# Carrying an angle from chunk to chunk: an accumulating DMA of one row in place of a second matmul

## The chip, the core and the metric

The kernel runs on one NeuronCore of a Trainium2 chip. The metric is the device time of one launch in microseconds (us), from the first to the last instruction with what lies around it. Five engines work side by side, each through its own instructions in order: TensorE (PE) multiplies matrices, VectorE (DVE) and ScalarE (ACT) work elementwise, GpSimd (POOL) does small elementwise work and issues some DMAs, SyncE (SP) issues the other DMAs. They wait for one another by semaphores only.

## The reference

Two blocks follow each other. The first is a gated linear recurrence with complex gates, for 4 batches, 8 heads, 768 time steps and head size 48:

```python
mag = np.sqrt(a_re * a_re + a_im * a_im)
scale = np.minimum(mag, 0.999) / (mag + 1e-06)
a = (a_re + 1j * a_im) * scale          # the reference keeps the two parts apart
for t in range(S):
    S_state = a[:, :, t, :, None] * S_state + einsum('bhd,bhe->bhde', k[:, :, t], v[:, :, t])
    y[:, :, t] = einsum('bhd,bhde->bhe', q[:, :, t], S_state.real)
```

The second is a mixer on `x`, the `y` of all heads side by side (batch, 768 tokens, 384 channels):

```python
h = x.transpose(0, 2, 1) @ U @ V         # over tokens, rank 32
u = x + h.transpose(0, 2, 1)
out = u + np.maximum(u @ w_ch1, 0.0) @ w_ch2    # 384 -> 1536 -> 384
```

All inputs and the output are float32.

## The kernel before, in words

The 768 tokens of a batch are cut into 6 chunks of 128, so there are 24 chunks over the 4 batches. Tokens lie on the 128 partitions and the 384 channels (8 heads of 48) on the free axis. Chunks go through the gate work in groups: chunk 0 alone, chunk 1 alone, and then pairs (2, 3), (4, 5) and so on to (22, 23).

**The gates** (`gate_steps`). A gate is a complex number; the recurrence needs the running product of gates, so the kernel adds logarithms of magnitudes and adds angles. Steps s0 to s2 make the log magnitude `l` and the ratio whose arctangent is the angle (ACT functions Square, Ln, Exp; DVE between them). `after_each` (L301) multiplies `l` with a triangle (`es`) and `of_blocks` (L309 to L320) with block sums (`tot`), after copying `l` twice into `ll`. Step s4 (L326 to L329) makes the angle of each token's gate, in turns: `y`. Step s5 (L331 to L340) adds these angles along time. For one chunk, TensorE multiplies `y` with the triangle `prefix`, which sums each token's angle with all earlier ones of the chunk (L336), into the PSUM tile `ph`. A chunk that isn't the first of its batch also needs the angle at the end of the chunk before. That is row 127 of `F[:, (i-1) % 2]`, and a second matmul into the same `ph` adds it to all 128 tokens, with the constant `tail` (zero but for -1 in its last row) as the stationary operand (L338). Then ACT adds the constant MAGIC, which rounds the turns to whole numbers (L339), and DVE takes the fraction (L340). The result `F` is the negative of the angle's fraction of a turn, hence the -1 in `tail`. Step s6 turns both chunks of the group at once into sines and cosines: `n` (L348), and two `cs` (L349, L350).

`F` has two slots, one for even and one for odd chunks; `y` and the other gate temporaries have one buffer each, so the next group's Square into `y` waits for the last `ph` matmul of this group.

**The chunks.** `prep_steps` multiplies q and k with `es` and `cs` (`qkc`, DVE), transposes them on TensorE (`tr`, L380) and copies them out on ACT. `chain_steps` builds the attention matrix of a chunk in levels: `inner` matmuls (L412) alternate with DVE multiplications of `QK` (the line of the helper `mul`, L256), then `place` copies, `corners` (L443), `corner` (L453), keys (`ks`, L479), outputs (`yT`, L465 and L469), the state update (`dk`, L485) and the transposed output (`yr`, L497), which ACT copies to the chunk's `x`.

**The mixer** (`mixer_steps`) works on pairs of chunks: rank (L540), mixed (L550), transposes `uT`, 12 `up` tiles (L563) with a ReLU on ACT (`h`), 2 `down` tiles (L571), an addition on DVE (L574) and the output DMA from POOL (L575).

**The order.** Python emits these steps interleaved (`weave`), from streams with a begin and an end within a chunk's turn; the tile framework then schedules the instructions and sets each engine's order and semaphores. The mixer of the first batch begins once that batch's 6 chunks are done. The last mixer pairs, of the last batch, run alone at the end. POOL's queue carries the constants at the start, the `ll` copies from chunk 8 on, and the 24 output DMAs. All loads are issued by SP.

Of the kernel before, what the change touches and what calls it, by code (L numbers as in the profile page):

```python
# [9 lines left out]
FP = mybir.dt.float32  # L10
I32 = mybir.dt.int32
U32 = mybir.dt.uint32
AF = mybir.ActivationFunctionType
OP = mybir.AluOpType
PSUM = bass.MemoryType.PSUM

CH = 128
# [3 lines left out]
GC = 2  # L21
# [14 lines left out]
def kernel(  # L36
# [24 lines left out]
    nc = tc.nc  # L61
# [3 lines left out]
    DM = H * D  # L65
# [9 lines left out]
    MAGIC = 12582912.0  # L75
# [10 lines left out]
    def pool(name, bufs, **kw):  # L86
        return ctx.enter_context(tc.tile_pool(name=name, bufs=bufs, **kw))

    singles = pool("singles", 1)
# [19 lines left out]
    def where(i):  # L109
        return divmod(i, NCH)  # L110
# [21 lines left out]
    prefix = singles.tile([128, CH], FP, name="prefix")  # L132
# [3 lines left out]
    ident = singles.tile([128, 128], FP, name="ident")  # L136
# [3 lines left out]
    def column(nm, value):  # L140
        t = singles.tile([128, 1], FP, name=nm)
        nc.vector.memset(t, value)
        return t

    leps, lmax, tiny = column("leps", math.log(1e-6)), column("lmax", LNMAX), column("tiny", 1e-30)
    magic, fourth = column("magic", MAGIC), column("fourth", 0.25)

    tail = singles.tile([128, CH], FP, name="tail")
    nc.gpsimd.tensor_scalar(out=tail, in0=ident[:, 127:128].to_broadcast([128, CH]), scalar1=-1.0, scalar2=None,
                            op0=OP.mult)  # L150

    after = singles.tile([128, CH], FP, name="after")
    quads = prefix.rearrange("p (b t) -> p b t", t=4)
# [1 line left out]
                            in0=quads[:, :, 3:4].to_broadcast([128, CH // 4, 4]), in1=quads, op=OP.subtract)  # L155
# [9 lines left out]
    F = singles.tile([128, GC, DM], FP, name="F")  # L165
# [75 lines left out]
    def act(o, i, f, **kw):  # L241
        return nc.scalar.activation(out=o, in_=i, func=f, **kw)  # L242
# [3 lines left out]
    def queue(ins):  # L246

        if queued:
            behind(ins, queued[-1])
        queued[:] = [ins]  # L250

    def tact(*a, **kw):
        queue(act(*a, **kw))

    def mul(o, a, b):
        nc.vector.tensor_tensor(out=o, in0=a, in1=b, op=OP.mult)  # L256

    def heads(a):
        return a.rearrange("p (x d) -> p x d", d=D)
# [4 lines left out]
    def gate_steps(g):  # L264
        st = {}
        lo, hi = GROUPS[g]
        W = (hi - lo) * DM

        def tmp(nm):
            st[nm] = pt.tile([128, GC * DM], FP, tag=nm, name=nm)[:, 0:W]  # L270
            return st[nm]

        def s0():
            x, y = tmp("x"), tmp("y")
            act(x, T["ar", g], AF.Square)
            act(y, T["ai", g], AF.Square)
            nc.vector.tensor_tensor(out=x, in0=x, in1=y, op=OP.add)
            nc.vector.tensor_scalar(out=x, in0=x, scalar1=M2LO, scalar2=M2HI, op0=OP.max, op1=OP.min)

        def s1():  # L280
            queue(nc.scalar.preload_act_table_set("natural_log_exp_and_others"))
            x, y, l, n = st["x"], st["y"], tmp("l"), tmp("n")
            act(n, T["ar", g], AF.Abs)
            tact(l, x, AF.Ln)
            tact(x, l, AF.Exp, scale=0.5)
            nc.vector.tensor_tensor(out=x, in0=x, in1=n, op=OP.add)
            tact(y, l, AF.Exp, scale=-0.5, bias=leps)
            tact(y, y, AF.Ln, bias=1.0)

            act(l, l, AF.Relu, scale=-0.5, bias=lmax)  # L290
            nc.vector.scalar_tensor_tensor(out=l, in0=l, scalar=LNMAX, in1=y, op0=OP.subtract, op1=OP.add)  # L291

        def s2():
            x = st["x"]
            tact(x, x, AF.Ln)
            tact(x, x, AF.Exp, scale=-1.0)
            mul(x, x, T["ai", g])

        def after_each(i):
            ps = psT.tile([128, DM], FP, tag="t", padded_shape=[128, 512], name="es")  # L300
            nc.tensor.matmul(out=ps, lhsT=after, rhs=st["l"][:, (i - lo) * DM:(i - lo + 1) * DM], start=True, stop=True)  # L301
            T["es", i] = pe.tile([128, 2, DM], FP, tag="es", name="es")
            tact(T["es", i][:, 0], ps, AF.Exp)
            tact(T["es", i][:, 1], ps, AF.Exp, scale=-1.0)

        def of_blocks(i):
            l = st["l"][:, (i - lo) * DM:(i - lo + 1) * DM]
            ll = pkc.tile([128, H, 2, D], FP, tag="ll", name="ll")
            (nc.scalar.copy if i < NCH + GC else nc.gpsimd.tensor_copy)(out=ll, in_=heads(l).unsqueeze(2).to_broadcast([128, H, 2, D]))  # L309
            if g == 0:  # L310
                queue(nc.scalar.preload_act_table_set("natural_log_exp_and_others"))
            ps = psT.tile([128, H, 64], FP, tag="t", name="tot")
            for h in range(H):
                nc.tensor.matmul(out=ps[0:D2, h, 0:NTOT], lhsT=ll[:, h].rearrange("p u d -> p (u d)"), rhs=total,  # L314
                                 start=True, stop=True)
            tt = pTT.tile([D2, H * NTOT], FP, tag="T", name="T")
            for n in SIZES:
                m = CH // n
                T["T", i, n] = tt[:, H * FIRST[n]:H * (FIRST[n] + m)].rearrange("p (h b) -> p h b", h=H)
                tact(T["T", i, n], ps[0:D2, :, FIRST[n]:FIRST[n] + m], AF.Exp, scale=-1.0)  # L320

        def s4():
            queue(nc.scalar.preload_act_table_set("trig_and_small"))
            x, y = st["x"], st["y"]

            act(y, T["ar", g], AF.Sign, bias=tiny)  # L326
            tact(x, x, AF.Arctan)
            nc.vector.scalar_tensor_tensor(out=y, in0=x, scalar=math.pi / 4, in1=y, op0=OP.subtract, op1=OP.mult)
            act(y, y, AF.Identity, scale=1.0 / math.pi, bias=fourth)  # L329

        def s5(i):  # L331

            f = F[:, i % GC]
            first = where(i)[1] == 0
            ps = psT.tile([128, DM], FP, tag="t", padded_shape=[128, 512], name="ph")
            nc.tensor.matmul(out=ps, lhsT=prefix, rhs=st["y"][:, (i - lo) * DM:(i - lo + 1) * DM], start=True, stop=first)  # L336
            if not first:
                nc.tensor.matmul(out=ps, lhsT=tail, rhs=F[:, (i - 1) % GC], start=False, stop=True)  # L338
            act(f, ps, AF.Identity, bias=magic)  # L339
            nc.vector.scalar_tensor_tensor(out=f, in0=f, scalar=MAGIC, in1=ps, op0=OP.subtract, op1=OP.subtract)  # L340

        def s6():
            cs = pg.tile([128, GC, H, 2, D], FP, tag="cs", name="cs")
            for i in range(lo, hi):
                T["cs", i] = cs[:, i - lo]
            cs = cs.rearrange("p c h u d -> p (c h) u d")[:, 0:W // D]
            f = F.rearrange("p c m -> p (c m)")[:, lo % GC * DM:lo % GC * DM + W]
            act(st["n"], f, AF.Abs)  # L348
            tact(cs[:, :, 1], heads(f), AF.Sin, scale=-2.0 * math.pi)  # L349
            tact(cs[:, :, 0], heads(st["n"]), AF.Sin, scale=-2.0 * math.pi, bias=quarter)  # L350

        each, blocks = ([lambda f=f, i=i: f(i) for i in range(lo, hi)] for f in (after_each, of_blocks))
        turns = [s4] + [lambda i=i: s5(i) for i in range(lo, hi)] + [s6]
        if g == 0:
            return [s0, s1, s2] + each, turns + blocks
        return [s0, s1, s2] + each + blocks, turns
# [251 lines left out]
    first = sum([mixer_steps(m, pu) for m in range((NT - NCH) // MC)], [])  # L608
# [83 lines left out]
```

## Time and profile before

| | |
|---|---|
| median of 3 runs (lowest to highest) | 881.14 us (879.32 to 882.34) |
| the profiled execution's own time | 880.63 us |
| its span, first to last instruction | 878.9 us |
| mean granted TensorE clock | 0.959 |
| ph matmul passes, L336 and L338 | 48 and 40 |
| DMA to HBM out of POOL's queue | 24, each 192 KB, 2.1 us to landing |

The profile is of one execution. "Busy" sums the time in which an engine executed; "x" gives a count. A float32 matmul shows as two instructions (passes), each with a weight load, which the profile lists as PEld and which overlaps other passes. Durations of matmuls include their way through the array, so back-to-back passes overlap in the records and the price of one more pass is read from a run of many. A line number with an arrow after a time, such as "[2.07 <-PE ph L338]", says how long the engine had been idle before the instruction and which instruction ended the wait.

### The profile page before, as it was taken

Reading aid. Unit: us, or ns where it says so; the run is one execution under the profiler, and the core shown is the slowest. Engines: PE = TensorE matmul, PEld = TensorE weight load, DVE = VectorE, ACT = ScalarE, POOL = GpSimd, SP = SyncE. Lnnn points to the kernel's source line nnn. Section 1 sums busy time; section 2 is a strip of 40 time slices with the busy share of each in tenths; the row PEclk is TensorE's granted clock in tenths of the full one; section 3 lists DMA queues with packets and bytes.
Section 4 is the critical chain, followed back from the end, with each engine's and each line's share of the span. In section 5 each row is a group of like instructions: output and inputs, shape, how many; then the busy total and the mean of one; then the engine's idle time right before and its main releaser. Section 6 shows DMA issues by size and latency. Waiting matters only on the chain.

```text
span 878.9 us, 24505 instructions
## 1 busy us (share of the span) xinstructions
PE 793.9 (90%) x11088; PEld 586.8 (67%) x11088; DVE 434.2 (49%) x621; ACT 465.2 (53%) x983; POOL 44.4 (5%) x67
## 2 busy tenths in 40 slices
PE   3657878888899999999999999999999999999997
PEld 2444656656677776866867867866867778575774
DVE  3577588789865635525536527427516343001010
ACT  7797787657654755745737628619615324020110
POOL 3000000010400000000000000000000000000000
PEclk9978879699899999999999999999999999999999
DMA  7442233242401400401301301301100000000000
GB/s 169 108 93 61 59 83 84 65 109 97 113 20 29 82 11 21 81 19 26 69 10 38 65 10 39 65 19 29 29 19 11 3 19 2 19 1 18 10 10 18
DMA packets 130904, 40.27 MB, mean 46 GB/s; under 512 B 126448, under 2 KB 127344, under 8 KB 130800
## 3 DMA queue, kind: packets, MB, share of 16 engines
q1 hardware_dynamic: 129264, 33.99, 17.4%
q0 software_dynamic: 1536, 4.72, 1.5%
q8 instruction: 87, 1.43, 0.7%
q14 instruction: 17, 0.14, 0.1%
HBM read 33.59 MB, written 4.72 MB: 44 GB/s over the span
## 4 chain that ended last, share of the span: by engine, by line
PE 75%; ACT 14%; DVE 6%; issue 3%; POOL 1%; DMA 0%; POOLq 0%; DVEq 0%; ACTq 0%
PE down L571 21%; PE up L563 19%; PE inner L412 6%; PE tot L314 4%; PE tr L380 4%; PE yT L465 4%; PE dk L485 3%; PE es L301 3%; PE yT L469 2%; PE ph L336 2%; PE ks L479 2%; ACT y L242 2%; DVE QK L256 1%; ACT n L242 1%; ACT cs L242 1%
## 5 line engine op out<-in xcount | busy, mean ns | idle before, releaser
L563 PE MATMUL up<-uT,w 128*128 128x256 f32 x864 | 210.6, 389 | 8.8 <-ACT h L242 5.5
L571 PE MATMUL down<-w,h 128*128 128x384 f32 x576 | 190.2, 487 | 0.0
L256 DVE TENSOR_TENSOR QK<-QK,T 96x1024 f32<-96x1024 f32 (+1 forms) x144 | 157.3, 1097 | 54.5 <-PE corners L443 38.1
L563 PEld LDWEIGHTS up<-uT,w 128*128 128x128 f32 x864 | 158.7, 192 | 33.5 <-ACT h L242 8.3
L571 PEld LDWEIGHTS down<-w,h 128*128 128x128 f32 x576 | 108.1, 190 | 71.3 <-issue 0.2
L574 DVE TENSOR_TENSOR x<-down,x 128x384 f32<-128x384 f32 x24 | 13.4, 557 | 215.3 <-PE down L571 215.3
L242 ACT ACTIVATE h<-up 128x256 f32<-128x256 f32 x144 | 55.0, 382 | 117.3 <-PE up L563 116.6
L382 ACT COPY QK<-tr 96x512 f32<-96x512 f32 x96 | 55.5, 582 | 73.5 <-PE tr L380 72.5
L412 PE MATMUL inner<-QK 96*32 96x32 f32 x6144 | 82.9, 203 | 10.8 <-DVE QK L256 5.3
L412 PEld LDWEIGHTS inner<-QK 96*32 96x32 f32 x6144 | 68.8, 114 | 34.9 <-issue 19.6
L380 PE MATMUL tr<-ident,qkc 128*96 128x128 f32 x384 | 66.0, 301 | 9.4 <-DVE qkc L256 8.1
L414 DVE COPY_PREDICATED DG<-mask,inner 128x256 f32<-128x256 int32 x96 | 42.3, 441 | 48.4 <-PE inner L412 46.9
L380 PEld LDWEIGHTS tr<-ident,qkc 128*96 128x96 f32 x384 | 45.1, 137 | 26.0 <-DVE qkc L256 9.5
L472 ACT COPY yTs<-yT 128x512 f32<-128x512 f32 x24 | 14.1, 587 | 81.2 <-PE yT L469 79.5
L465 PE MATMUL yT<-AT,VP 128*64 128x128 f32 x384 | 47.1, 303 | 3.0 <-ACT AT L457 1.5
L256 DVE TENSOR_TENSOR qkc<-qk,cs 128x768 f32<-128x768 f32 x48 | 44.5, 949 | 2.7 <-PE tr L380 1.9
L314 PEld LDWEIGHTS tot<-total,ll 128*96 128x96 f32 x384 | 39.0, 178 | 9.2 <-POOL ll L309 4.0
L314 PE MATMUL tot<-total,ll 128*96 128x63 f32 x384 | 40.7, 262 | 4.5 <-POOL ll L309 2.7
L437 ACT COPY AT<-DG 32x256 f32<-32x256 f32 x96 | 38.4, 400 | 9.1 <-DVE DG L414 8.2
L309 POOL COPY ll<-l 128x768 f32<-128x768 f32 x16 | 22.9, 1428 | 400.4 <-DVE l L291 256.8
L301 PE MATMUL es<-l,after 128*128 128x384 f32 x48 | 26.0, 633 | 12.8 <-DVE l L291 12.6
L465 PEld LDWEIGHTS yT<-AT,VP 128*64 128x64 f32 x384 | 28.8, 148 | 12.5 <-issue 9.3
(93 smaller groups left out, 949.4 us busy)
## 6 DMA issues: line engine op xcount, KB each, us to landing
ar<-in_a_re_dram SPq DMA_DIRECT2D x24, 192.0 KB, 3.5
ai<-in_a_im_dram SPq DMA_DIRECT2D x24, 192.0 KB, 3.2
qk<-in_q_dram SPq DMA_DIRECT2D x24, 192.0 KB, 2.9
qk<-in_k_dram SPq DMA_DIRECT2D x24, 192.0 KB, 3.4
VP<-in_v_dram SPq DMA_DIRECT2D x24, 192.0 KB, 2.6
raw<-in_moe_w_ch_dram SPq DMA_DIRECT2D x6, 768.0 KB, 4.6
raw<-in_moe_w_ch_dram SPq DMA_DIRECT2D x12, 384.0 KB, 3.7
out_dram<-x POOLq DMA_DIRECT2D x24, 192.0 KB, 2.1
```

Source lines behind the costliest of these rows:

```text
L242: return nc.scalar.activation(out=o, in_=i, func=f, **kw)
L256: nc.vector.tensor_tensor(out=o, in0=a, in1=b, op=OP.mult)
L301: nc.tensor.matmul(out=ps, lhsT=after, rhs=st["l"][:, (i - lo) * DM:(i - lo + 1) * DM], start=True, stop=True)
L314: nc.tensor.matmul(out=ps[0:D2, h, 0:NTOT], lhsT=ll[:, h].rearrange("p u d -> p (u d)"), rhs=total, start=True, stop=True)
L380: nc.tensor.transpose(out=ps[0:D2, j], in_=T["qkc", i][:, u, hh * HH + j].rearrange("p u d -> p (u d)"), identity=ident)
L382: nc.scalar.copy(out=T["QK", i][:, u, hh * HH:(hh + 1) * HH], in_=ps[0:D2])
L412: nc.tensor.matmul(out=ps[js, h], lhsT=k_of(h)[:, js], rhs=q_of(h)[:, js], start=True, stop=True, tile_position=(0, j * BLK))
L414: T["level"] = nc.vector.copy_predicated(out=DG[i % 2], mask=mask[:, n].unsqueeze(1).to_broadcast([128, H, BLK]), data=ps)
L437: nc.scalar.copy(out=AT[i % 2][js, :, js], in_=DG[i % 2][js])
L465: nc.tensor.matmul(out=y[u * DP:(u + 1) * DP, p], lhsT=vv[:, h], rhs=AT[i % 2][:, h], start=True, stop=(c == 0), tile_position=(0, u * DP))
L563: nc.tensor.matmul(out=ps, lhsT=w1[:, f, ff * 128:(ff + 1) * 128], rhs=st["uT"][:, f], start=(f == 0), stop=(f == KD - 1))
L571: nc.tensor.matmul(out=ps, lhsT=st["h"][:, ff, cc * CH:(cc + 1) * CH], rhs=w2[:, ff], start=(ff == 0), stop=(ff == KF - 1))
```

## The change

The tail matmul (L338) and its constant go. Instead, for every chunk that isn't the first of its batch, a DMA from POOL's queue adds row 127 of the last chunk's `F` to row 0 of this chunk's `y`, before the prefix matmul: what is in the first token's increment reaches all 128 tokens of the sum. The row is 384 numbers, 1.5 KB. For this `F` now holds the angle's fraction itself, not its negative: ACT takes `-ph` plus MAGIC, DVE adds `ph` where it took it away, and the sine's scale changes sign. There are 20 such chunks (24, less the first of each batch).

```diff
-    tail = singles.tile([128, CH], FP, name="tail")
-    nc.gpsimd.tensor_scalar(out=tail, in0=ident[:, 127:128].to_broadcast([128, CH]), scalar1=-1.0, scalar2=None,
-                            op0=OP.mult)
...
         def s5(i):
             f = F[:, i % GC]
-            first = where(i)[1] == 0
+            y = st["y"][:, (i - lo) * DM:(i - lo + 1) * DM]
+            if where(i)[1] > 0:
+                nc.gpsimd.dma_start(out=y[0:1], in_=F[CH - 1:CH, (i - 1) % GC], accum_op=OP.add)
             ps = psT.tile([128, DM], FP, tag="t", padded_shape=[128, 512], name="ph")
-            nc.tensor.matmul(out=ps, lhsT=prefix, rhs=st["y"][:, (i - lo) * DM:(i - lo + 1) * DM], start=True, stop=first)
-            if not first:
-                nc.tensor.matmul(out=ps, lhsT=tail, rhs=F[:, (i - 1) % GC], start=False, stop=True)
-            act(f, ps, AF.Identity, bias=magic)
-            nc.vector.scalar_tensor_tensor(out=f, in0=f, scalar=MAGIC, in1=ps, op0=OP.subtract, op1=OP.subtract)
+            nc.tensor.matmul(out=ps, lhsT=prefix, rhs=y, start=True, stop=True)
+            act(f, ps, AF.Identity, scale=-1.0, bias=magic)
+            nc.vector.scalar_tensor_tensor(out=f, in0=f, scalar=MAGIC, in1=ps, op0=OP.subtract, op1=OP.add)
...
-            tact(cs[:, :, 1], heads(f), AF.Sin, scale=-2.0 * math.pi)
+            tact(cs[:, :, 1], heads(f), AF.Sin, scale=2.0 * math.pi)
```

The scheduler orders the changed program anew, so other instructions change places too. In the changed program's order on POOL, the 20 row DMAs stand among the `ll` copies and the output DMAs; on TensorE the `ph` matmuls of a pair, which stood close together before in some groups, have other work between them, and those of chunks 2 and 4 stand later among the work of the chunks before.

## The prediction

> **What bounds the kernel now.** I read in this order: the busy shares, the busy times by stretch, what TensorE waits for, the phase tile, the time order around it.
>
> ```profile
> PE 793.9 (90%) x11088; PEld 586.8 (67%) x11088; DVE 434.2 (49%) x621; ACT 465.2 (53%) x983; POOL 44.4 (5%) x67
> ```
>
> The average hides two regimes. By stretch (us, then busy us and instructions of PE, weight loads, DVE, ACT, POOL, then granted clock):
>
> ```profile
> 0.00:216.00 216.00, 158.51 (x2886) 115.41 (x2886) 154.54 (x231) 160.98 (x320) 10.59 (x29) 0.86 0.39 92
> 216.00:770.00 554.00, 536.38 (x7820) 400.48 (x7821) 271.30 (x376) 290.44 (x628) 30.56 (x32) 0.99 0.15 35
> 770.00:879.00 109.00, 99.05 (x383) 70.86 (x383) 8.36 (x15) 13.83 (x36) 3.24 (x6) 1.00 0.03 11
> ```
>
> Until 216 us no engine is full (PE 73%, DVE 72%, ACT 75%): chains from engine to engine set the pace. From 216 to 770 us TensorE is 97% busy and no other engine passes 52%; what is taken from it there shortens the run. After 770 us the change issues nothing. The phase tile (duration min/median/max, first and last start):
>
> ```profile
> L338 PE MATMUL ph<-F,tail x40: 486/486/847, 39.8 to 657.3; 128*128 128x384 f32 x40
> L242 ACT ACTIVATE F<-ph,magic x24: 562/581/582, 16.9 to 657.8; 128x384 f32<-128x384 f32 x24
> L340 DVE SCALAR_TENSOR_TENSOR F<-F,ph x24: 542/553/559, 17.5 to 658.4; 128x384 f32<-128x384 f32 x24
> ```
>
> Forty rows are 20 tail matmuls in two passes each. 486 ns is latency; the price in a full queue is read from the chain, where passes of the same shape run back to back:
>
> ```profile
> 771.07 15.81 PE up L563 x72
> 786.87 15.48 PE down L571 x48
> ```
>
> So a 128x384 pass costs 15.48/48 = 0.3225 us, a matmul of two passes 0.645; an "up" matmul of two passes costs 15.81/36 = 0.44. The time order on ACT for the pair of chunks 2 and 3 shows how the tail stands in a serial chain:
>
> ```profile
> 65.54 0.94 ACT L242 ACTIVATE y<-y,fourth 128x768 f32<-128x768 f32 x1
> ...
> 69.78 0.58 ACT L242 ACTIVATE F<-ph,magic 128x384 f32<-128x384 f32 x1 [2.07 <-PE ph L338]
> ...
> 71.96 0.58 ACT L242 ACTIVATE F<-ph,magic 128x384 f32<-128x384 f32 x1 [0.27 <-PE ph L338]
> ...
> 73.95 0.85 ACT L242 ACTIVATE n<-F 128x768 f32<-128x768 f32 x1
> ```
>
> From the end of y (66.48) to n, the first reader of both finished chunks, 7.5 us pass. Read likewise: chunk 1 alone 4.2 us (38.28 to 42.51), chunks 4 and 5 10.2 (101.61 to 111.85), 6 and 7 11.1 (144.93 to 156.03), 8 and 9 6.0 (208.02 to 214.02).
>
> **What the Trainium skill says.** DMA: Bandwidth & Descriptors, "SWDGE vs HWDGE vs iDMA": accumulation in a DMA must be issued from GpSimd; so POOL's queue carries it. The same page, "Anatomy of one DMA — SWDGE (gpsimd) path": about 2.0 us fixed plus bytes over 436 GB/s, most of it the write's receipt. The trace agrees for the one POOL transfer it has, though that goes to HBM and doesn't accumulate:
>
> ```profile
> out_dram<-x POOLq DMA_DIRECT2D x24, 192.0 KB, 2.1
> ```
>
> TensorE: Matmul & The Clock Gate, "Step-by-step: what each phase is for": matmuls stay in program order and only weight loads are pulled ahead, so a matmul that waits for a DMA holds every later one. The trace agrees in kind: waits stand ahead of single matmuls with later work queued. SBUF — State Buffer, "Who interferes with whom": DVE and GpSimd exclude each other on a shared port pair for a whole instruction; POOL's ll copy shows it, 0.83 us at best and 6.64 us at worst. The out_dram issue, 0.54 us at the median and 0.77 at most, shows little of it.
>
> **The change part by part.**
>
> Removed: 20 tail matmuls. Chunks 1 to 5 and 7 (six) lie before 216 us. Fourteen belong to chunks 8 to 11, 13 to 17 and 19 to 23; 8 and 9 stand at 208 to 213 us, where the mixer's matmuls have begun to fill the queue. 14 x 0.645 = **9.0 us** of TensorE. Their weight loads run beside other passes, so they are worth nothing more. The tail tile's setup, one POOL instruction of 1.1 us at 5.1 us, gates no first matmul: POOL makes "after", which the first es needs, ahead of it. Worth nothing. The sign moves into ACT's scale and DVE's add: same instructions, 0.58 and 0.55 us, same shapes.
>
> Added: 20 DMAs of 1.5 KB (in the built program 16 runs of 24 numbers each). POOL pays 20 x 0.54 = 10.8 us in an engine 95% idle: nothing on the path. Issue to landing isn't in this trace for such a transfer: low end 2.0 us (the fixed part above; no reason for less), high end 3.5 (the slowest median row of the loads, ar, as the SDMA engines are 39% busy early). I take 2.1.
>
> Added waits. The first chunk of a group now runs y, DMA, ph; the second runs F of the first, DMA, ph. A pair is then 2.1 + ph 0.8 + F 0.58 + 0.55 + 2.1 + 0.8 + 0.58 + 0.55 + about 0.6 for hops = 8.7 us from y to n with warm passes, 9.0 with the first one cold. Against the measured spans:
> - Chunk 1: 0.1 + 2.1 + 1.65 (a cold ph) + 0.58 + 0.56 + 0.3 = 5.3 against 4.2: +1.1.
> - Chunks 2, 3: 9.0 against 7.5: +1.5.
> - Chunks 4, 5: 9.0 against 10.2: fits, 0. Chunks 6, 7 (one DMA): 7.4 against 11.1: fits, 0.
> - Chunks 8, 9: 8.7 against 6.0: 2.7 later, but TensorE has "up" work between.
>
> Behind a waiting ph stands the next row of TensorE; behind F on ACT stand the place copies and the next group's Square; behind the DMA on POOL stand ll copies (tot waits for these) and output stores (nobody does).
>
> Where the cover is: the built order keeps the ph matmuls apart now. Between ph(8) and ph(9) stand 15 inner at 0.02, 9 up at 0.44 and 8 corner at 0.086: 0.3 + 4.0 + 0.7 = 5.0 us of matmul time, against F 0.58 + 0.55 + DMA 2.1 + hops 0.3 = 3.5. For the later second chunks the same count gives 20 to 22 us, or 10.7 where a group straddles two batches' work; for first chunks 4.5 to 15 us after the last matmul that y can depend on. So after 216 us I cost the new waits at 0. Without that cover each would cost up to 3.5 us.
>
> Moved: before 120 us the built order puts ph(2) behind yT, dk, yr and a whole inner level of chunk 0/1, and ph(4) behind yr, where both stood ahead of them. I take +1.0 for this, bounds 0 and +14.7: dk began 6.3 us after ph(2) did (73.36 against 67.06), yr 8.4 after ph(4) (110.78 against 102.33). I take so little because work that is moved ahead (corners, place copies) needn't be done later.
>
> Given back: TensorE waited 22 of 652 us after 216; a shorter queue meets its producers sooner. I take 10% of the gain, 0.9 (0 to 2).
>
> Sum: -9.0 + 1.1 + 1.5 + 1.0 + 0.9 = **-4.5 us**. The profiled run took 880.63 us (span 878.9 and 1.7 around it), so it would take 876.1; the median of the runs, 881.14, is 0.5 above that run, so I forecast 876.6.
>
> **The rivals.**
> - *Everything early is hidden as well.* ACT idles 55 us before 216, so the 2.6 us may vanish: -9.0, or 872. With cold passes also saved (a tail of 1.35 us at 68.39) 869 is the low end.
> - *The DMA takes 3.5 us.* Chunk 1 +2.5, chunks 2 and 3 +4.3, chunks 4 and 5 +1.6: 8.4, with 1.9 given back and moved, against 9.0: +1.3, or 882.4. Chunks 8, 9 then need 4.9 of their 5.0 us. For it: loads land in 2.6 to 3.5 us. Against it: the row is tiny and stays in SBUF.
> - *Slower: the early order.* TensorE keeps its order, so ph(2) and ph(4), put behind yr, start when yr is done; cs, qkc and everything for the next chunks shift. At its full price 14.7 + 0.9 - 9.0 = +6.6, or 887.7. It decides from 60% of its price on, 9 us. For it: in the trace qkc starts at 76.38, 0.03 us after cs ends, so that group's chain had no slack. Against it: for chunks 4 and 5 cs ended at 114.25 and qkc started at 115.97.
> - *It doesn't do what it says:* excluded; in the built order no tail matmul is left and 20 row transfers stand on POOL.
>
> **How the numbers follow.** 0.3% (2.6 us) is about what a measurement of this kernel can tell from no change. Forecast with the first rival: 0.50, all faster. The slow DMA, or an early order at half its price: within 0.3%, 0.17. The early order at over three quarters, alone or with the slow DMA: 0.33, slower. I leave that much because the early stretch is a net of short chains whose order has changed throughout. Range 869 to 888: from the first rival's low end to the full price of the third. The likeliest case's own range is 872 to 878.5.
>
> **What would show it.** Right: no L338 rows; PE busy down by 11 to 20 us; y row transfers landing in 2.0 to 2.5 us; PE waits on them after 216 us under 2 us in all; 216 us's events 1 to 5 us later; the rest about 9 us shorter. Wrong: ph waits of over 1 us for a DMA late in the run, landing above 3 us, ACT idle ahead of F up by several us before 120 us, or the first mixer "up" over 8 us later than 205.8.

## The result and the profile after

Side by side on one chip, four runs each, the changed kernel took 882.38 us (881.51 to 884.08) and the kernel before 880.52 (879.32 to 882.34). The ratio is 1.0022, interval 0.9997 to 1.0046: no change that can be measured. It lies inside the predicted range (869 to 888), but the likeliest case, 4.5 us faster, did not come. A second pairing later (`after_again` below) gave 0.9999 [0.9973, 1.0026], with medians of 884.49 and 882.47 us. Every ratio here is taken over all runs but those more than 1.5% slower than their kernel's fastest, and so isn't the quotient of the two medians.

The profiled run of the changed kernel took 881.51 us, span 879.7, at a granted clock of 0.959 as before. Its busy line answers to the first one shown:

```profile
PE 786.9 (89%) x11048; PEld 586.2 (67%) x11048; DVE 437.8 (50%) x621; ACT 464.5 (53%) x983; POOL 55.7 (6%) x86
```

The 40 passes of the tail are gone, and TensorE is busy 7.0 us less (786.9 for 793.9). Yet the span is 0.9 us longer. The same three stretches of the changed kernel (columns as before: us, then PE, weight loads, DVE, ACT, POOL, granted clock):

```profile
0.00:216.00 216.00, 154.16 (x2828) 116.42 (x2828) 150.20 (x222) 156.19 (x314) 15.15 (x35) 0.87 0.38 91
216.00:770.00 554.00, 533.88 (x7840) 399.06 (x7840) 279.26 (x385) 294.44 (x633) 37.36 (x45) 0.99 0.15 35
770.00:879.00 109.00, 98.88 (x383) 70.70 (x381) 8.37 (x15) 13.83 (x36) 3.24 (x6) 0.99 0.03 11
```

Before 216 us fewer matmuls are done than before (2828 passes instead of 2886; at most 16 of these are tails): the kernel is behind. In the middle TensorE idles 20.1 us (554 less 533.88) where it idled 17.6. The new instructions, from the list of the phase tile `ph` (a "phase" below is a `ph` matmul) (duration in ns min/median/max, first and last start) and from the page's list of DMAs (KB each, median us from issue to landing):

```profile
L335 PE MATMUL ph<-y,prefix x48: 486/488/1010, 15.1 to 657.1; 128*128 128x384 f32 x48
L333 POOL DMA_DIRECT2D y<-F x20: 757/766/984, 38.5 to 638.5; - x20
```

```profile
y<-F POOLq DMA_DIRECT2D x20, 1.5 KB, 1.9
```

The tail rows are gone, the 20 row transfers are there, and one lands in 1.9 us at the median (1.8 to 4.0; three take 3.4 or more, those of chunks 1 and 8 and one at 571.86 us).

**Where the time went** is read from the chain of waits, which runs through the mixer's second "down" tile of every pair once TensorE is full. Its entries for the first, third and eighth pair (start us, us, what), before:

```profile
265.54 7.74 PE down L571 x24
...
393.41 7.74 PE down L571 x24
...
704.45 7.74 PE down L571 x24
```

and in the changed kernel:

```profile
268.54 7.74 PE down L568 x24
...
395.97 7.74 PE down L568 x24
...
704.28 7.74 PE down L568 x24
```

The changed kernel is 3.0 us behind at the first pair, 2.6 at the third, and 0.2 ahead at the eighth. So the full stretch gave back 3.2 us, where 11 tail matmuls of 0.645 us, 7.1 us, had gone, and the loss before it took as much. (The price holds: in the trace of the kernel before, each of these 11 tails holds the next pass of TensorE back by 0.645 us.) This division of the run is used for all kernels below, so here are all of them, from one trace each. The columns: start of `n` of chunks 2 and 3; start of the first "up" pass; from there to the first pass of pair 1's second "down"; from there to pair 8's; from the last "down" pass to the end of the span; the span; the number of row transfers. (The chain enters a tile 0.16 us after its first pass starts.)

| kernel | n(2,3) | first up | to pair 1 | to pair 8 | after the last pass | span | DMAs |
|---|---|---|---|---|---|---|---|
| before | 73.9 | 205.76 | 59.62 | 438.91 | 5.58 | 878.9 | 0 |
| after | 84.5 | 210.69 | 57.69 | 435.74 | 6.63 | 879.7 | 20 |
| after_again | 84.6 | 213.90 | 57.59 | 436.14 | 6.63 | 883.2 | 20 |
| no_carry | 75.0 | 209.53 | 50.54 | 435.48 | 5.56 | 870.1 | 0 |
| no_carry_again | 75.5 | 206.42 | 50.54 | 435.51 | 5.57 | 867.0 | 0 |
| both | 83.9 | 216.90 | 57.29 | 438.97 | 6.62 | 888.8 | 20 |
| late_dma | 73.9 | 207.20 | 56.39 | 435.66 | 6.16 | 874.4 | 14 |
| dma_4up | 76.8 | 206.43 | 56.09 | 435.76 | 6.38 | 873.7 | 17 |
| dma_2up | 80.3 | 212.03 | 57.82 | 436.06 | 6.55 | 881.5 | 19 |
| dma_only1 | 77.1 | 209.67 | 58.79 | 438.58 | 5.63 | 881.7 | 1 |
| before_split | 75.0 | 220.06 | 52.37 | 438.89 | 5.55 | 883.6 | 0 |
| after_split | 80.5 | 217.85 | 52.43 | 433.80 | 6.62 | 877.4 | 20 |
| late_split | 73.8 | 213.65 | 52.58 | 434.18 | 6.16 | 873.3 | 14 |
| dma4_split1 | 74.1 | 203.03 | 53.13 | 444.08 | 6.38 | 873.4 | 17 |

The part left out, pair 8 to the last "down" pass, is 169.0 us in every kernel without "split" and 166.7 in those with it. Two executions of one kernel differ by 3.1 and 3.2 us at the first "up" and by at most 0.4 in every later column. So the later columns can be compared from one trace, the early ones only roughly; for these the times of all runs decide (14 runs of after_again lie between 876.3 and 886.0, so two traces don't show the whole spread). In the split kernels the mixer's order around the first pairs is another. There the first "up" and the way to pair 1 are compared as a sum, and in dma4_split1 the way to pair 8 is part of that sum too.

For these two traces, then, the 0.9 us are: +4.9 before the first "up", -1.9 to pair 1, -3.2 to pair 8, +1.1 after the last pass.

### The profile page after: what moved, and what is told of

The parts are those of the page before. It is cut to its first block, busy times and chain, and to the rows that moved or that the text cites. A ratio compares the mean times of both kernels' runs of the same rounds, so it can differ in the third digit from the quotient of the medians.

```text
span 879.7 us, 24520 instructions
## 1 busy us (share of the span) xinstructions
PE 786.9 (89%) x11048; PEld 586.2 (67%) x11048; DVE 437.8 (50%) x621; ACT 464.5 (53%) x983; POOL 55.7 (6%) x86
## 4 chain that ended last, share of the span: by engine, by line
PE 71%; ACT 18%; DVE 4%; issue 3%; DMA 2%; POOL 0%; SPq 0%; POOLq 0%; DVEq 0%; ACTq 0%
PE down L568 21%; PE up L560 17%; PE inner L409 5%; PE tot L310 4%; PE tr L377 3%; PE yT L462 3%; PE dk L482 3%; ACT y L238 3%; PE es L297 2%; PE yT L466 2%; ACT x L238 2%; PE ph L335 2%; ACT l L238 2%; ACT L277 2%; ACT n L238 1%
## 5 line engine op out<-in xcount | busy, mean ns | idle before, releaser
L409 PEld LDWEIGHTS inner<-QK 96*32 96x32 f32 x6144 | 71.1, 116 | 37.7 <-issue 22.5
L409 PE MATMUL inner<-QK 96*32 96x32 f32 x6144 | 85.1, 205 | 11.9 <-DVE QK L252 8.3
L377 PE MATMUL tr<-ident,qkc 128*96 128x128 f32 x384 | 68.6, 311 | 13.0 <-DVE qkc L252 11.2
L377 PEld LDWEIGHTS tr<-ident,qkc 128*96 128x96 f32 x384 | 48.1, 143 | 30.3 <-DVE qkc L252 10.7
L310 PEld LDWEIGHTS tot<-total,ll 128*96 128x96 f32 x384 | 42.4, 191 | 8.0 <-POOL ll L305 2.9
L310 PE MATMUL tot<-total,ll 128*96 128x63 f32 x384 | 44.1, 276 | 3.2 <-POOL ll L305 1.7
L462 PE MATMUL yT<-AT,VP 128*64 128x128 f32 x384 | 44.3, 296 | 0.2
L466 PE MATMUL yT<-QK,G 96*48 96x128 f32 x320 | 35.5, 286 | 0.0
L335 PE MATMUL ph<-y,prefix 128*128 128x384 f32 x48 | 23.6, 578 | 13.2 <-DMA y<-F 8.2
```

Source lines behind the costliest of these rows:

```text
L377: nc.tensor.transpose(out=ps[0:D2, j], in_=T["qkc", i][:, u, hh * HH + j].rearrange("p u d -> p (u d)"), identity=ident)
L409: nc.tensor.matmul(out=ps[js, h], lhsT=k_of(h)[:, js], rhs=q_of(h)[:, js], start=True, stop=True, tile_position=(0, j * BLK))
L462: nc.tensor.matmul(out=y[u * DP:(u + 1) * DP, p], lhsT=vv[:, h], rhs=AT[i % 2][:, h], start=True, stop=(c == 0), tile_position=(0, u * DP))
L466: nc.tensor.matmul(out=y[u * DP:u * DP + D, p], lhsT=T["G"][:, h], rhs=q_of(h), start=False, stop=True, tile_position=(0, u * DP))
```

## The experiments

Every ratio is against the kernel before in the same pairing, with its 95% interval.

**late_dma** has the transfers from chunk 8 on alone; chunks 1 to 5 and 7 keep their tail matmul, with +1 since `F` has changed sign.

```diff
+    tail = singles.tile([128, CH], FP, name="tail")
+    nc.gpsimd.tensor_scalar(out=tail, in0=ident[:, 127:128].to_broadcast([128, CH]), scalar1=1.0, scalar2=None,
+                            op0=OP.mult)
...
-            if where(i)[1] > 0:
+            first = where(i)[1] == 0
+            dma = i >= 8
+            if dma and not first:
                 nc.gpsimd.dma_start(out=y[0:1], in_=F[CH - 1:CH, (i - 1) % GC], accum_op=OP.add)
...
-            nc.tensor.matmul(out=ps, lhsT=prefix, rhs=y, start=True, stop=True)
+            nc.tensor.matmul(out=ps, lhsT=prefix, rhs=y, start=True, stop=first or dma)
+            if not (first or dma):
+                nc.tensor.matmul(out=ps, lhsT=tail, rhs=F[:, (i - 1) % GC], start=False, stop=True)
```

> The row DMA only for chunks 8 to 23; chunks 1 to 5 and 7 keep the second matmul (with +1 in the tail's last row, as F has its new sign). Parting theory: the change loses about 4.9 us before the first up matmul (it starts at 210.7 instead of 205.8) and gains about the same after it. Then the first up starts at 205 to 207 here, the time from it to the end is 668 to 670, and the run takes 876 to 877, 4 to 5 us under the kernel before. Rival, that the early loss comes from the order being set anew and not from the DMA chain: the first up stays near 210 and the run at 881 to 882.

Measured: 877.58 us against 882.01, ratio 0.9946 [0.9923, 0.9968]. The early order is that of before again (n of chunks 2 and 3 at 73.9), and the loss before the first "up" shrinks from 4.9 to 1.4 us. The late columns are the changed kernel's. The run is 4.4 us under the kernel before, and the forecast was 4 to 5. So replacing the late tails by transfers pays, and the early transfers lose it again.

**no_carry** has neither transfer nor tail: it leaves the carried angle out.

```diff
-            if where(i)[1] > 0:
-                nc.gpsimd.dma_start(out=y[0:1], in_=F[CH - 1:CH, (i - 1) % GC], accum_op=OP.add)
```

> Neither the DMA nor the second matmul: the angle of the last chunk's end is left out, so this prices the removal alone. In the built order the second group of uT transposes stands right behind the second mixed matmul, as in the changed kernel. Order theory (the late gain of 7.1 us of TensorE is eaten by uncovered waits at mixed and uT, and not by the DMA): down blocks between 265 and 704 us gain only about 3 us, as in the changed kernel, with waits of uT for DVE x of 8 us on TensorE and its weight loads each; the run is 4 to 7 us under the kernel before. Rival, waits for the DMA: without it the late stretch gains the full 7 us and the run is 9 us or more under the kernel before.

Measured: 867.8 us, ratio 0.9831 [0.9775, 0.9887]; the span of the profiled run was 870.1. From pair 1 to pair 8 it takes 435.48, as good as the changed kernel's 435.74: there the transfers are hidden, as forecast, and even with no carry at all only 3.4 of 7.1 us come back. To pair 1 it takes 50.54, 7.2 us less than the changed kernel: there the transfers are not hidden. The run is 14 us under the kernel before, where 4 to 7 were forecast; in the traces 9.1 of them lie on the way to pair 1 (59.62 to 50.54).

**both** has the transfers and a second matmul whose stationary operand is all zeros, so that the tail's time is there and adds nothing.

```diff
+            first = where(i)[1] == 0
-            nc.tensor.matmul(out=ps, lhsT=prefix, rhs=y, start=True, stop=True)
+            nc.tensor.matmul(out=ps, lhsT=prefix, rhs=y, start=True, stop=first)
+            if not first:
+                nc.tensor.matmul(out=ps, lhsT=tail, rhs=F[:, (i - 1) % GC], start=False, stop=True)
```

> The DMA as in the changed kernel, and beside it a second matmul per chunk with an all-zero tail, so TensorE's work is that of the kernel before, and its late order too (in the built order corners stand between the second mixed and its uT). It prices the DMA alone. Order theory: the late stretch is as before (down blocks from 265 to 704 us take 439 us, within 0.5), the early one loses 5 to 8 us, and the run is 886 to 889. Rival, the DMA's waits cost late: the stretch from 265 to 704 us is 3 us or more longer than before, and the run over 889.

Measured: 890.58 us (886 to 889 forecast), ratio 1.0074 [1.0035, 1.0114]. With before, after and no_carry it completes a square of four. From pair 1 to pair 8: tail without transfers 438.91, tail with them 438.97, no tail 435.48 and 435.74. That column is set by the tail alone. To pair 1 only the kernel with neither is quick: 50.54 against 57.29 to 59.62.

**after_split** is the changed kernel with the mixer's step "mixed" emitted as two: both additions first, then both transposes `uT`.

```diff
-            if cc == 0:
-                st["uT"] = pu.tile([128, KD, N], FP, tag="uT", name="uT")
...
+        def flip(cc):
+            if cc == 0:
+                st["uT"] = pu.tile([128, KD, N], FP, tag="uT", name="uT")
+            u = T["x", i0 + cc]
...
-        for cc in range(MC):
-            add(mixed, cc)
+        for f in (mixed, flip):
+            for cc in range(MC):
+                add(f, cc)
```

The reason to try it lies in the time order at the turn from one chunk group to the next. In the kernel before, on TensorE (start us, us, line, op, tiles, count; idle time before it in brackets):

```profile
343.04 0.81 PE L550 MATMUL mixed<-r,V 128*128 128x384 f32 x2
...
343.93 0.66 PE L443 MATMUL corners<-QK 96*32 96x32 f32 x29
...
344.87 0.55 PE L555 MATMUL uT<-ident,x 128*128 128x128 f32 x3
```

and in the changed kernel:

```profile
345.77 0.81 PE L547 MATMUL mixed<-r,V 128*128 128x384 f32 x2
347.23 0.55 PE L552 MATMUL uT<-ident,x 128*128 128x128 f32 x3 [0.65 <-DVE x L549]
348.36 0.63 PE L440 MATMUL corners<-QK 96*32 96x32 f32 x26 [0.58 <-DVE QK L252]
```

`uT` transposes what DVE makes of `mixed`. Before, corner matmuls stood between the two and covered DVE. Without the tail the scheduler puts `uT` straight behind `mixed`; TensorE waits for DVE, and the corners, no longer ahead of it, wait as well. The largest waits of TensorE between the first and the eighth pair (us in total, times, longest), before:

```profile
PE up L563 <- ACT h L242: 4.5, 6, 0.8
PE tr L380 <- DVE qkc L256: 1.8, 6, 0.3
PE corners L443 <- DVE QK L256: 1.2, 3, 0.7
PE uT L555 <- DVE x L552: 1.0, 2, 0.6
PE inner L412 <- ACT ks L480: 0.4, 2, 0.2
```

and in the changed kernel:

```profile
PE corners L440 <- DVE QK L252: 4.2, 7, 0.7
PE uT L552 <- DVE x L549: 4.0, 6, 0.7
PE inner L409 <- ACT ks L477: 3.0, 4, 0.8
```

The last three rows of before have grown from 2.6 us to 11.2, and the first two, 6.3, are gone. No transfer is among them. In the order of no_carry these places are the same as here, and its rows are the same to the digit; those of both are the ones of before (`up` 4.5, `tr` 1.8, `corners` 1.2). So it is the tail's absence that brings the new order and its waits about, not the transfer.

> The changed kernel, with the mixer's mixed step emitted as two: both mixed matmuls with their additions first, then both groups of uT transposes with their copies. In the built order an inner level and yr or tr stand between a mixed matmul and the uT that needs it. Order theory: the waits of uT for DVE x on TensorE fall from 8.1 us to under 3, the stretch from 265 to 704 us gains some 3 to 4 us on the changed kernel, and the run takes 877 to 880. Rival, waits for the DMA: 881 to 883, as the changed kernel.

Measured: 881.81 against 882.01, ratio 0.9972 [0.9940, 1.0004]; the forecast of 877 to 880 was missed. The waits of TensorE between pairs 1 and 8 in after_split:

```profile
PE corners L440 <- DVE QK L252: 4.1, 7, 0.6
PE up L563 <- ACT h L238: 1.8, 2, 0.9
PE inner L409 <- ACT ks L477: 1.7, 4, 0.6
```

The row of `uT` is gone, that of `inner` nearly halved, and one of `up` is back. The stretch falls from 435.74 us to 433.80 (3 to 4 us were forecast), and the idle time in it to what it was before: 9.7 us (434.0 less 424.3 busy), where the changed kernel has 11.9 and before 9.8. A further 2.3 us come out of the end, where no tails are. Against this, pair 1 is reached 1.9 us later (270.28 for 268.38), which is within what two executions of one kernel differ by. So the wait is real and worth about 2 us of the missing 3.9 in the full stretch; the total isn't told apart from no change.

**before_split** is the same edit in the kernel before.

> The kernel before with the mixed step emitted as two and nothing else. Order theory (the split mends what the removed tail laid open): in the kernel before TensorE waited only 1.0 us for DVE x between 265 and 704 us, so that stretch stays at 438 to 439 us and only the last mixer pairs gain, 2 to 2.5 us; 879 to 881 us. Rival, that the split is a gain of its own: the stretch shrinks by 2 us or more here too, and the run is 877 or less.

Measured: 881.16 against 881.61, ratio 0.9989 [0.9969, 1.0009]. Its full stretch takes 438.89, with the edit, and 438.91 without: where `uT` was covered, separating it gains nothing. That is the control for after_split.

**late_split** is late_dma with the split.

> The row DMA for chunks 8 to 23 only, with the mixed step emitted as two: both edits that gained, together. If they add up: the second down of the first mixer pair at 264 to 266 us, 434 us from there to that of the eighth pair as in after_split (438.9 before), and 2 us less at the end; 874 to 876 us, 6 to 8 us under the kernel before. If they don't add up, because each sets the order anew: 877 to 880.

Measured: 876.61 against 881.61, ratio 0.9941 [0.9923, 0.9958]; stretch 434.18, so 1.5 us less than late_dma, but not told apart from it in time (0.9946), and just beyond the 874 to 876 of two gains that add up.

**dma_2up**, **dma_4up** and **dma_only1** are late_dma with another line, to place the early price:

```diff
-            dma = i >= 8
+            dma = i >= 2
```

> The row DMA for all chunks but chunk 1, which keeps the second matmul. Against the changed kernel it prices chunk 1's DMA, against dma_4up those of chunks 2 and 3. The prediction's terms, +1.1 for chunk 1 and +1.5 for 2 and 3, would put the second down of the first mixer pair at 267.3 us (268.4 in the changed kernel, 263.6 with late_dma). If chunk 1's wait costs what its path grew by (3.1 us from y to n), 265.3.

```diff
-            dma = i >= 8
+            dma = i >= 4
```

> The row DMA from chunk 4 on; chunks 1 to 3 keep the second matmul. The prediction costs the DMAs of chunks 4, 5 and 7 at nothing: then the second down of the first mixer pair stands where late_dma has it, at 263.6 us within 0.7. If they cost a share like the others of the 4.8 us between late_dma and the changed kernel, it stands at 265 or later.

```diff
-            dma = i >= 8
+            dma = i == 1
```

> The row DMA for chunk 1 alone; all other chunks keep the second matmul. It prices the first of the early waits by itself. The prediction's term is +1.1 us: 882 to 883 beside the kernel before at 881.6. From the medians of the changed kernel and of the one without chunk 1's DMA the price is 5 us (0.6%): 886 to 887. If it only shifts the start and the rest follows, n of chunk 1 starts about 3 us later than 42.51 and the first up 3 to 5 us later than 205.76.

Measured: dma_2up 879.27, 0.9963 [0.9941, 0.9986]; dma_4up 876.44, 0.9930 [0.9901, 0.9959]; dma_only1 880.27, 0.9991 [0.9969, 1.0012]. From chunk 4 on the transfers cost nothing early (first "up" at 206.43; the ratio is no worse than late_dma's). With chunks 2 and 3 the first "up" is at 212.03, and pair 1's second "down" at 269.85, later than either forecast (267.3 or 265.3). Chunk 1's transfer alone puts its `n` 2.7 us later (45.16 for 42.51) and shows no loss in time (880.27, where 882 to 883 or 886 to 887 were forecast); yet dma_2up, without it, is if anything better than the changed kernel, with it (0.9963 against 0.9999, intervals that overlap). So how the early loss divides between chunk 1 and chunks 2 and 3 stays open.

**dma4_split1** is dma_4up with the split for all mixer pairs but the very first (`m` counts the pairs of all batches).

```diff
+        if m == 0:
+            for cc in range(MC):
+                add(mixed, cc)
+        else:
+            for f in (add_rank, flip):
+                for cc in range(MC):
+                    add(f, cc)
```

> The row DMA from chunk 4 on, and the mixed step emitted as two for all mixer pairs but the first, which stands among the last chunks without mixer work. If the gains add: the early stretch as in dma_4up (second down of the first pair near 262.5 us), 434 us from there to the second down of the eighth pair and 2.25 us less at the end, so 872 to 874 us, 8 to 10 us under the kernel before. If the split costs early what it saves late, as in late_split: 876 to 878.

Measured: 879.69 against 881.85, ratio 0.9966 [0.9944, 0.9987]. It adds nothing to dma_4up, and both forecasts, 872 to 874 and 876 to 878, were missed.

**after_again** and **no_carry_again** repeat two kernels in one pairing, so that the whole price of the transfers is read from runs taken side by side.

> The changed kernel itself, again, beside the next one on the same chip, as its early stretch varies with the granted clock. Expected 1.000 to 1.004 of the kernel before, with the stretch from the second down of the first pair to that of the eighth at 435.7 us once more. If it comes out like the kernels with the DMA from chunk 2, 4 or 8 on (0.993 to 0.996), the early price that they seemed to show is noise.

> Without DMA and without second matmul, again (the carried angle is left out), for a narrower interval on what the removal alone is worth and, against the changed kernel beside it, on what the DMAs cost in all. From the first look: 0.983 to 0.988 of the kernel before, so a price of 10 to 15 us for 20 DMAs, all of it before 265 us; the later stretch 435.5 us. If the price is only that of the traced early stretches, 8 us, the two kernels stand 0.009 apart.

Measured: 884.49 (14 runs), ratio 0.9999 [0.9973, 1.0026], and 864.26 (6 runs), ratio 0.9778 [0.9740, 0.9815]. The transfers cost 0.9999 - 0.9778 = 2.2%, some 19 us by the ratios; taking the tails away is worth as much. The price is above the 10 to 15 us that were forecast. The two traces differ by 16.2 us: 7.5 before the first "up", 7.0 to pair 1, 0.6 to pair 8, 1.1 at the end. The first pair of traces gave 1.2, 7.2, 0.3 and 1.1. Only the first term varies. Some 9 of the 19 us are thus placed; by the ratios the other 10 or 11, an estimate, are lost before the first "up", where single traces can't place them.

**What happens on the way to pair 1.** Between the first "up" and pair 1's second "down" after and no_carry do the same matmuls, tile by tile, and each takes its time twice alike (57.69 and 57.59; 50.54 and 50.54). In this stretch lie the phases of chunks 8 and 9. In the changed kernel, all engines, with other rows left out:

```profile
213.23 0.76 POOL L333 DMA_DIRECT2D y<-F  x1 [11.39 <-ACT h L238]
...
217.28 1.28 PE L335 MATMUL ph<-y,prefix 128*128 128x384 f32 x2 [1.92 <-DMA y<-F]
...
220.06 0.76 POOL L333 DMA_DIRECT2D y<-F  x1 [6.07 <-DVE F L337]
...
224.82 0.81 PE L335 MATMUL ph<-y,prefix 128*128 128x384 f32 x2
...
227.24 0.85 ACT L238 ACTIVATE n<-F 128x768 f32<-128x768 f32 x1
...
233.53 0.61 PE L377 MATMUL tr<-ident,qkc 128*96 128x128 f32 x4 [1.36 <-DVE qkc L252]
...
236.25 1.08 PE L409 MATMUL inner<-QK 96*32 96x32 f32 x64 [2.11 <-DVE QK L252]
...
237.99 1.65 PE L297 MATMUL es<-l,after 128*128 128x384 f32 x2 [0.65 <-DVE l L287]
```

The first phase waits 1.92 us for its row. This row is the slowest of the 20: it lands 4.0 us after its issue (3.7 in after_again, 4.2 in late_dma), where 1.9, the median, would have come just before TensorE ran out of work at 215.36. Why it is slow there was not tried; SP issues four weight loads from 212.87 on. The second phase stands 7.5 us behind the first on TensorE, and starts 2.9 us after its own row has landed (221.91), so `n` starts 16.6 us after the first "up" (210.69). What `n` leads to is late as well: `tr`, `inner` and `es` wait 4.1 us together. In no_carry both phases run in one go and `n` follows 6.1 us after the first "up" (209.53):

```profile
212.22 1.45 PE L333 MATMUL ph<-y,prefix 128*128 128x384 f32 x4
...
215.67 0.85 ACT L238 ACTIVATE n<-F 128x768 f32<-128x768 f32 x1
...
222.80 1.04 PE L375 MATMUL tr<-ident,qkc 128*96 128x128 f32 x8
```

The idle times account for 2.8 of the 7.2 us (6.7 us idle against 3.9, summed over the gaps in the stretch). The rest is busy time: the same passes keep TensorE busy 4.4 us longer, at a lower granted clock. The whole stretch and ten us of it, same columns as above, the column after POOL being the clock; changed kernel:

```profile
210.69:268.38 57.69, 50.97 (x766) 38.59 (x767) 50.29 (x71) 36.73 (x78) 6.05 (x7) 0.91 0.29 74
235.00:245.00 10.00, 8.09 (x164) 6.74 (x164) 8.97 (x14) 8.47 (x17) 1.02 (x1) 0.67 0.70 173
```

no_carry:

```profile
209.53:260.07 50.54, 46.59 (x767) 36.15 (x767) 48.38 (x69) 36.90 (x77) 4.38 (x3) 1.00 0.31 81
235.00:245.00 10.00, 8.76 (x184) 7.16 (x183) 9.24 (x15) 4.93 (x21) 2.24 (x1) 1.00 0.63 144
```

The Trainium skill, TensorE: Matmul & The Clock Gate, "Part 1: The HAM clock gate", says that the clock follows how busy the array has just been, and this trace agrees: after the gaps before 236.25, `es` takes 1.65 us for its two passes, where no_carry's take 0.81 at 235.74. The kernel before has a hole of its own there, TensorE busy 5.6 of 10 us from 215 to 225 and then a clock of 0.75, and takes 59.62: three tails more (1.9 us by the price), and the rest idle time and clock. What makes that hole with tails was not tried. Nor was it tried how the 7.2 us divide between the wait for the row and the order that keeps the two phases apart: no kernel here has the transfers and both phases in one place.

## Why the prediction was right or wrong

| term | forecast | trace of after | after_again |
|---|---|---|---|
| before the first "up" (chunk 1, chunks 2 and 3, order) | 1.1 + 1.5 + 1.0 = +3.6 | +4.9 | +8.1 |
| to pair 1: 3 tails; (8,9) at 0 | -1.9 | -1.9 | -2.0 |
| to pair 8: 11 tails, less "given back" | -7.1 + 0.9 = -6.2 | -3.2 | -2.8 |
| after the last pass | 0 | +1.1 | +1.1 |
| sum | -4.5 | +0.9 | +4.4 |

The medians of the two pairings stand 1.9 and 2.0 us above the kernel before, nearer the first trace. The range, 869 to 888, held, but not by its argument: the likeliest case, "faster" at 0.50, failed, and the result fell among those within 0.3%, given 0.17. Of the two reasons named there, the slow transfer is out at the median, and of the 5.4 us by which the first trace misses the sum, 3.0 are in the third row and only 1.3 in the first.

**The step that failed: "given back, 10% of the gain, 0.9 (0 to 2)".** It was 3.9 us of 7.1 from pair 1 to pair 8, outside its own bounds. The argument was that a shorter queue meets its producers sooner, in proportion to the waits of before. In fact the scheduler, with one matmul less, put `uT` straight behind `mixed`, and 8.6 us of waits on DVE and ACT are new there while 6.3 us of others went. I had compared the built orders around `ph` alone. after_split, with before_split as its control, shows that taking `uT`'s wait away is worth 1.9 us. The other 2.0 don't show as idle time, since TensorE's idle time is back at 9.7 us there; but a delay shorter than the record of the pass before, which overlaps the next, isn't listed as idle. Counted from the start of each pass to the start of the next, less the median of this interval for its tile and shape in the two traces, the delays between pairs 1 and 8 add up to 38.1 us before, 42.1 in the changed kernel, 41.8 in no_carry and 40.1 in after_split. That is the whole 3.9: 9.6 us more ahead of `inner`, `corners` and `uT`, 6.9 less ahead of `up` and `tr`, and 1.2 more elsewhere. In no_carry each of the five differs by the same amount to within 0.05 us, so these are the places, and the transfer isn't the cause. The bare price times the count was right as a count (no tail is left) and wrong as a gain.

**"Chunks 8, 9: 2.7 later, but TensorE has 'up' work between, 0": right in the net, wrong inside.** The path from y to n took 14.3 us, not 8.7, and the transfers cost 7.2 us against no_carry in this stretch. The removal was worth 9.1 there, not 1.9. The two errors cancel, which is luck. The cover of 5.0 us that I counted between the phases did stand there; it didn't cover what mattered: the second phase comes after its cover and not when its row has landed, and what hangs on `n` is late by all of it. The sign that I had named, PE waits on the DMA after 216 us under 2 us in all, was met and was the wrong meter. The changed kernel's only such row after 216 us:

```profile
PE ph L335 <- DMA y<-F: 1.9, 1, 1.9
```

It is one wait of 1.9 us, and the stretch lost 7.2: the rest of the price appeared as waits on DVE and as clock.

**Early terms: the total about right, by luck in the parts.** The first "up" came 4.9 us later (8.1 in the repeat), inside the 1 to 5 that I gave and then beyond them. The path of chunk 1 cost 3.0 (n at 45.51 for 42.51), not 1.1, since its row took 3.4 us from issue at 38.54 to landing at 41.95. For chunks 2 and 3, n started 10.6 us later (84.55 for 73.95). Of this, 8.0 are that y itself ended later (74.44 for 66.48), and 2.6 are the longer path from y to n. The third rival, `ph` of chunk 2 held back behind other work of TensorE, is not what the trace shows: it starts at 77.36, 0.4 us after its row landed. A later y is in part the new order without the tail: no_carry, with no transfer at all, starts y 4.8 us later than the kernel before (70.29 for 65.54) and makes up for it with a path of 3.8 us. Here is the serial chain in the changed kernel:

```profile
74.75 0.77 POOL L333 DMA_DIRECT2D y<-F  x1 [35.23 <-ACT y L238]
...
77.36 0.91 PE L335 MATMUL ph<-y,prefix 128*128 128x384 f32 x2
...
79.77 0.76 POOL L333 DMA_DIRECT2D y<-F  x1 [4.25 <-DVE F L337]
...
81.65 1.65 PE L335 MATMUL ph<-y,prefix 128*128 128x384 f32 x2 [3.07 <-DMA y<-F]
```

From the end of y to n 10.1 us pass, not the 9.0 forecast: the second phase runs slow, 1.65 us for 0.81. The forecast's own sum was short as well: with one slow phase at the 1.65 that it used for chunk 1, its 8.7 becomes 9.5 and not 9.0. But 7.4 of the 10.6 were gone again by n of chunks 6 and 7 (159.24 for 156.03), so the reason to take the order's price low, that work moved ahead needn't be done later, held in the main.

**The landing** was taken at 2.1 and is 1.9; the rival of 3.5 us is out for the median, but it came true where it hurt: chunk 1 took 3.4 us and chunk 8 4.0. **POOL's issue** takes 0.77, not 0.54: 15.8 us in all, off the path as said. The reading of the slow `ll` copy of 6.64 us (225.49 to 232.13 in the kernel before) fits the trace: DVE works without a break until 231.44, and the copy at 306.14, with DVE idle, takes 0.83; no run here tests it. **PE busy down by 11 to 20** was wrong (7.0): busy time is a union of overlapping records whose length depends on the clock, so it doesn't count passes. **After the last pass** I had nothing; see the last section.

**Versions better than both.** Transfers from chunk 4 on (0.9930 [0.9901, 0.9959]), from chunk 8 on (0.9946 [0.9923, 0.9968]), and the latter with the split (0.9941 [0.9923, 0.9958]) are 0.5 to 0.7% faster than the kernel before, and so than the changed one (0.9999 and 1.0022), whose intervals lie above theirs; their own overlap and don't rank them. They keep the matmul where short chains set the pace and use the transfer where TensorE is full, which is the split that the two regimes of the first profile suggest.

## What to carry to other kernels

Where an engine is full, an instruction taken out is worth its price only if what closes up behind it is ready: compare the built order of before and after at the place where the queue closes, and look for a consumer that now stands straight behind its producer. A transfer's cost is not the time that anyone waits for it; follow the tile that it delays to the first engine that runs out of work, and count the clock lost after the gap. One change may pay in a full stretch and lose in a serial one, so try it by stretch before judging it as a whole.

## What the runs showed of the hardware

Each row transfer adds some 0.05 us after the last pass, though none of them is near the end. What grows is one instruction of POOL at the program's closing line, a DRAIN that starts with POOL's last issue; the profile lists it with the sequencer and doesn't count it as busy. From the lists of that line, before and changed (duration in ns min/median/max of three):

```profile
L687 POOLq DRAIN  x3: 40/102/3187, 874.9 to 878.6; - x3
```

```profile
L684 POOLq DRAIN  x3: 46/112/4224, 874.7 to 879.5; - x3
```

By the number of row transfers the longest DRAIN takes 3.17 to 3.19 us (none, four traces), 3.23 (1), 3.76 (14), 3.98 (17), 4.14 (19) and 4.22 to 4.23 (20), and 0.8 us after its end the span is over. The time from the last pass to the end of the span grows alike, from 5.55 to 6.63. What the DRAIN does for each transfer stays open.

A transfer of 1.5 KB within the core that accumulates took 1.9 us at the median to land, little less than the 2.1 to 2.2 of the 192 KB output; its issue held POOL longer (0.77 us against 0.54).
